# Agent attention and maxout FFN on one core: two key groups of the start turned another way, and the loads behind them

## The chip, the cores and the metric

The kernel runs on one NeuronCore of a Trainium2 chip. The metric is the device time of one execution in microseconds (us). Before the change the median of 12 runs is 464.67 us, from 464.09 to 465.64. The engines named below are TensorE (PE; PEld is its weight load), VectorE (DVE), ScalarE (ACT), GpSimd (POOL) and SyncE (SP), which here issues nearly all DMAs.

## What is computed

Agent attention is followed by a maxout feed-forward layer. Four batches have 12544 rows of 128 channels each; there are 49 agents a batch and 768 hidden units.

```python
a2k = sm(agents, k)          # softmax(scale * agents @ k^T)
agent_v = a2k @ v            # 49 x 128 for each batch
q2a = sm(q, agents)          # softmax(scale * q @ agents^T)
x = (q2a @ agent_v).reshape(B * S, D)
h = np.maximum(np.maximum(x @ w1, x @ w2), x @ w3)
return (h @ w_out).astype(np.float32)
```

Inputs and output are float32. The kernel works in bf16 on TensorE.

## The kernel before

Since `x` is a product with only 49 rows of `agent_v`, the kernel multiplies those by the weights first: for each batch it makes `G`, 49 rows wide enough for the hidden units, and every row of q then needs only its 49 exponentials times `G`.

**Stages.** Batch 0 has a pass of its own over its keys and values ("early" groups). After that the kernel runs over 49 q groups of 1024 rows, numbered s = 0 to 48. Most of the first 36 "host" a key group of the next batch: while q group s is worked through, up to 1152 rows of k and v (nine blocks of 128) are cast, scored and added up, so that `G` of the next batch is ready at its border. The last batch's q groups host nothing.

**A key group** (`k_group`) has these steps: `load` (k, then v, by SyncE, into one of 14 buffers called st), `cast_k` and `cast_v` to bf16 on GpSimd (L280, L287), `turn_k`, which transposes the keys, `scores` (L312, TensorE), `exps` (L317, ScalarE), `values` (L323, TensorE), and two additions. `turn_k` has two forms. The TensorE form writes nine transposes into a PSUM tile (L294), and `evacuate` copies that to the SBUF tile kT on VectorE (L300). The DMA form is one transposing DMA issued by SyncE (L296) from the cast keys k_bf to kT. Early groups and groups 0 to 2 take the TensorE form, all later ones the DMA form.

**A q group** (`q_group`) loads q (L474), casts it on GpSimd (L478), turns it on TensorE (L483) with a copy to qT (L489, VectorE; for group 0 half of it on ScalarE, L491), and makes scores (L504) and exponentials (L510). Then come six hidden slices, f = 0 to 5. For each, TensorE makes u (`first`) and v (`second`), both L530; ScalarE turns u to a (`relu_first`, L545); VectorE takes the maximum with v, called x (L555). Slice 3 works in one tile: ScalarE's a3 (L542) is written in place, v3 is added to it, and ScalarE makes the result (L553). In what follows u0 is u of slice 0, and so on. Last, TensorE multiplies by the output weights (L560, L569), VectorE scales (L576) and SyncE stores (L583).

**Order.** Each step is put on a list with a time of its own (`at`), in units of which a group has six; the tables `KEY`, `BEGIN` and others hold the offsets. `emit` sorts the list and issues in that order, holding a step back until what it needs has been issued. The order on every engine's queue, SyncE's included, follows from it. SyncE issues in order, so a DMA that waits for a cast holds up the loads behind it.

**The rings.** Hidden slices, products for `G` (L418, copied by L423 for batch 0) and the TensorE form of `turn_k` take turns in three PSUM buffers (ring "uv"). Scores, q turns, output tiles and some filler matmuls (L254, which keep TensorE busy) share two buffers of another ring ("om"). SBUF holds three each of k_bf, kT and q_bf.

`last_key` is the time of the last early group, -2.804. The step that turns the keys of hosted groups is set at the end of `k_group`:

Of the kernel before, what the change touches and what calls it, by code (L numbers as in the profile page):

```python
# [16 lines left out]
def kernel(  # L17
# [83 lines left out]
    def table(s):  # L101
        if s + 1 in tails:
            return BORDER
        return BEGIN if s in tails and s < SB else KEY if s < SB else LATE
# [6 lines left out]
    def uv_tile(dtype=FP32):  # L111
        return psum.tile([P, 2, 512 if dtype == FP32 else 1024], dtype, tag="uv", bufs=3, name="uv_ps")
# [6 lines left out]
    def at(key, fn, name=None, needs=(), ring=None, frees=()):  # L119

        ops.append((key, len(ops), fn, name, needs, ring, frees))
# [61 lines left out]
    def load_tile():  # L185
        return loads.tile([P, KT, C], FP32, tag="st", name="st")
# [77 lines left out]
    def k_group(b, t0, n, key, s):  # L264

        d = {}
        early = s is None
        K = None if early else table(s)
        if s == 0:
            key += BEHIND  # L270

        def load():
            for name, src in (("k", k), ("v", v)):
                t = d[name] = load_tile()
                nc.sync.dma_start(t[:, :n, :], src[b, t0 * P:(t0 + n) * P, :].rearrange(
                    "(p j) c -> p j c", j=n))

        def cast_k():
            d["kb"] = work.tile([P, KT, C], BF16, tag="k_bf", bufs=3, name="k_bf")
            nc.gpsimd.tensor_copy(out=d["kb"][:, :n, :], in_=d["k"][:, :n, :])  # L280

        def cast_v():
            d["vb"] = work.tile([P, KT, C], BF16, tag="v_bf", bufs=4, name="v_bf")
            if early:
                nc.scalar.activation(d["vb"][:, :n, :], d["v"][:, :n, :], AF.Copy)  # L285
            else:
                nc.gpsimd.tensor_copy(out=d["vb"][:, :n, :], in_=d["v"][:, :n, :])  # L287

        def turn_k():
            d["kT"] = work.tile([P, KT, P], BF16, tag="kT", bufs=3, name="kT")  # L290
            if early or s < 3:
                t = d["kT_ps"] = uv_tile(BF16).rearrange("p i c -> p (i c)")
                for j in range(n):
                    nc.tensor.transpose(t[:, j * P:(j + 1) * P], d["kb"][:, j, :], ident)  # L294
            else:
                nc.sync.dma_start_transpose(out=d["kT"][:, :n, :],  # L296
                                            in_=d["kb"][:, :n, :].rearrange("p j c -> p (j c)"))

        def evacuate():
            nc.vector.tensor_copy(out=d["kT"][:, :n, :].rearrange("p j c -> p (j c)"),  # L300
                                  in_=d["kT_ps"][:, :n * P])

        def scores():
            if early:
                d["pair"] = uv_tile()
                d["s"] = d["pair"][:, 0, :]
                last_tile["t"] = d["s"]
            else:
                d["s"] = host[s]
            t = d["s"]  # L310
            for j in range(n):
                nc.tensor.matmul(t[:, j * A:(j + 1) * A], d["kT"][:, j, :], agT[:, b, :A],  # L312
                                 start=(j == 0), stop=True, skip_group_check=True)

        def exps():
            d["e"] = work.tile([P, KT * A], BF16, tag="e_k", bufs=3, name="e_k")
            nc.scalar.activation(d["e"][:, :n * A], d["s"][:, :n * A], AF.Exp, scale=scale)  # L317

        def values():
            t, c = (d["pair"][:, 1, :], 0) if early else (d["s"], CV)  # L320
            for j in range(n):
                e = d["e"][:, j * A:(j + 1) * A]
                nc.tensor.matmul(t[:, c:c + A], d["vb"][:, j, :], e, start=(early and j == 0),  # L323
                                 stop=True, skip_group_check=True)
                if early:
                    nc.tensor.matmul(t[:, A:2 * A], ones_bf, e, start=False, stop=True,
                                     skip_group_check=True)

        def add_values():
            w = 2 * A if early else A  # L330
            src = d["pair"][:, 1, :w] if early else d["s"][:, CV:CV + A]
            if t0 + n == NT and not early:
                nc.vector.tensor_tensor(out=avT[:, b, :A], in0=src, in1=Vacc[b], op=ALU.add)
            elif t0:
                nc.vector.tensor_tensor(out=Vacc[b], in0=src, in1=Vacc[b], op=ALU.add)
            else:
                Vacc[b] = work.tile([P, w], FP32, tag=f"Vacc{w}", name="Vacc")
                nc.vector.tensor_copy(out=Vacc[b], in_=src)

        def add_exps():  # L340
            if t0:
                nc.gpsimd.tensor_tensor(out=Eacc[b][:, :n * A], in0=Eacc[b][:, :n * A],  # L342
                                        in1=d["e"][:, :n * A], op=ALU.add)
            else:
                Eacc[b] = work.tile([P, KT * A], FP32, tag="Eacc", name="Eacc")
                nc.gpsimd.tensor_copy(out=Eacc[b], in_=d["e"])

        if early:
            g = ("early", t0)
            at(key - 30, load)  # L350
            at(key - 5, cast_k)
            at(key - 4, cast_v)
            at(key, turn_k, ("kt", g), (), "uv", [("kt_out", g)])
            at(key + 0.5, evacuate, ("kt_out", g), [("kt", g)])

            last = [("normalise", 0)] if t0 + n == NT else []
            late = max(0, (key - last_key) / 6 + 2)
            at(min(key + 6.6, last_key + 0.58 + 0.02 * late), scores, ("ks", g), [("kt_out", g)],
               "uv", [("ka", g)] + last)
            at(min(key + 7, last_key + 0.64 + 0.01 * late), exps, ("ke", g), [("ks", g)])  # L360
            done = last_key + (0.6 + 0.1 * late if late >= 1 else 0.55)
            at(min(key + 13.2, done), values, ("kv", g), [("ke", g)])
            at(min(key + 13.6, done + 0.01), add_values, ("ka", g), [("kv", g)])
        else:
            at(6.0 * s - 24.6, load)
            at(max(6.0 * s - 12.6, last_key - 3.4 + 0.2 * s), cast_k, ("k_cast", s))
            at(max(6.0 * s - 10.6, last_key - 3.3 + 0.2 * s), cast_v, ("v_cast", s))
            if s > 2:
                at(max(key - 9.1, last_key - 3.2), turn_k, ("kt_out", s), [("k_cast", s)])
            else:  # L370

                turn = 6.0 * s - 3.3 if s else KEY["v0"] + 0.01
                at(turn, turn_k, ("kt", s), (), "uv", [("kt_out", s)])
                at(turn + 0.05, evacuate, ("kt_out", s), [("kt", s)])
            at(key + K["ks"], scores, ("ks", s), [("kt_out", s), ("ho", s)])
            at(key + K["ke"], exps, ("ke", s), [("ks", s)])
            at(key + K["ke"] + 1.5, add_exps, ("kx", s), [("ke", s)])
            at(key + K["kv"], values, ("kv", s), [("ke", s), ("v_cast", s)])
            at(key + K["ka"], add_values, ("ka", s), [("kv", s)])
# [71 lines left out]
    def q_group(s):  # L451
# [3 lines left out]
        key = 6.0 * s  # L455
# [132 lines left out]
        def put(name, fn, *needs, ring=None, frees=()):  # L588
            at(key + K[name] + (BEHIND if s == 0 and name in ("sum", "rec") else 0), fn, (name, s), needs,
               ring, frees)  # L590
# [3 lines left out]
        if s == 0:  # L594
            at(last_key - 29.9, load)
            at(last_key - 3.5, cast)
            at(last_key + 0.76, turn_q, ("qt", 0), (), "om", [("qe", 0)])
            at(last_key + 0.77, evacuate, ("qe", 0), [("qt", 0)])
            at(last_key + 0.94, scores, ("s", 0), [("qe", 0)], "om", [("ex", 0)])
            at(last_key + 0.941, exps, ("ex", 0), [("s", 0)])  # L600
        elif not q_dma:
            at(key - 26, load)
            at(max(key - 12.8, last_key - 3.45 + 0.2 * s), cast, ("q_cast", s))
            put("qt", turn_q, ("q_cast", s), ring="om", frees=[("qe", s)])
            put("qe", evacuate, ("qt", s), *([("s", s - 3)] if s >= 3 else []))
        else:
            at(key - 32, load)
            at(key - 14.3, cast)
            at(key - 12.3, turn_q_dma, ("qe", s))
# [46 lines left out]
    last_key = KEY["u0"] - 2  # L656
# [19 lines left out]
    for b in range(1, B):  # L676
        for g in range(NK):
            s = (b - 1) * NT // GT + g
# [41 lines left out]
```

The softmax here doesn't subtract the row's maximum and nothing guards it: scores larger than these inputs give would overflow.

## Time and profile before

| | |
|---|---|
| median of 12 runs | 464.67 us |
| the profiled execution | 464.82 us |
| its span, first to last instruction | 463.0 us |
| granted TensorE clock, mean | 0.999 |
| busiest groups: maximum (L555, VectorE) | 297.2 us, x245, 1221 ns each |
| ReLU (L545, ScalarE) | 240.8 us, x245, 1026 ns each |
| hidden slices (L530, TensorE) | 187.2 us, x1248 |
| DMA moved | 118.26 MB, mean 255 GB/s |
| key transposes by DMA (L296) | x30, median 5.2 us to landing |

All durations come from one profiled execution; the 1.8 us between its time and its span lie outside the first and last instruction. Busy shares are means over stages with different limits. Rows of a timeline give start, length, engine, line, operation, what it writes and reads, and in brackets how long the engine stood idle before it and what ended that. A row named SPq is the issue of a DMA; its landing is a separate time. "Issue" in the chain of waits is time in which the engine waited for nothing that the profile shows.

### The profile page before, as it was taken

How to read it: one execution, taken by the hardware profiler on the slowest of the kernel's cores; microseconds unless marked ns; L12 is line 12 of the kernel's file. 1: busy time of each engine (PE TensorE's matmuls, PEld its weight loads, DVE VectorE, ACT ScalarE, POOL GpSimd, SP SyncE). 2: the span in 40 equal slices, each digit the busy share in tenths (PEclk: the TensorE clock that was granted, in tenths of full speed). 3: DMA queues.
4: the chain of work that ended last, by engine and by line, in shares of the span. 5: the costliest groups of instructions: out<-in, count | busy, mean ns of one | idle time of the engine just before them, and what ended most of it. 6: DMA issues, size and time to landing. Idle time of an engine off the chain costs nothing.

```text
span 463.0 us, 13350 instructions
## 1 busy us (share of the span) xinstructions
PE 438.2 (95%) x5473; PEld 274.4 (59%) x5473; DVE 403.1 (87%) x512; ACT 396.2 (86%) x460; POOL 171.2 (37%) x179
## 2 busy tenths in 40 slices
PE   2597899999999999999999999999999999999995
PEld 2465466666665666666656666666656555555554
DVE  3255899999988999999989999999988999999995
ACT  3365889989899899899999998998999999999991
POOL 2244963553452545536272446353240101000000
PEclk9999999999999999999999999999999999999999
DMA  8999999996999899997997999986766486644122
GB/s 313 407 411 391 409 361 323 347 323 145 315 302 310 289 243 309 346 271 241 300 317 259 278 328 294 291 258 188 175 138 187 132 192 153 177 120 124 60 93 92
DMA packets 81449, 118.26 MB, mean 255 GB/s; under 512 B 55207, under 2 KB 56683, under 8 KB 81387
## 3 DMA queue, kind: packets, MB, share of 16 engines
q1 hardware_dynamic: 81184, 117.30, 82.4%
q8 instruction: 43, 0.70, 0.6%
q14 instruction: 19, 0.16, 0.1%
q10 hardware_dynamic: 203, 0.10, 0.1%
HBM read 78.74 MB, written 25.69 MB: 226 GB/s over the span
## 4 chain that ended last, share of the span: by engine, by line
PE 80%; DMA 8%; DVE 4%; ACT 4%; issue 2%; SPq 0%; POOL 0%; DVEq 0%; ACTq 0%
PE uv_ps L530 34%; PE o_ps L569 29%; PE o_ps L560 6%; DMA st<-in_k_dram 5%; PE m_ps L483 4%; PE m_ps L504 3%; DVE r L555 3%; ACT a_sb L545 2%; DMA st<-in_q_dram 2%; DMA st<-in_v_dram 2%; PE m_ps L323 2%; PE m_ps L312 1%; PE m_ps L518 1%; DVE o_sb L576 1%; ACT uv_ps L542 0%
## 5 line engine op out<-in xcount | busy, mean ns | idle before, releaser
L555 DVE TENSOR_TENSOR r<-uv_ps,a_sb 128x1024 bf16<-128x1024 f32 x245 | 297.2, 1221 | 14.7 <-PE uv_ps L530 6.5
L545 ACT ACTIVATE a_sb<-uv_ps 128x1024 bf16<-128x1024 f32 x245 | 240.8, 1026 | 14.9 <-PE uv_ps L530 13.6
L530 PE MATMUL uv_ps<-e_q,G 49*128 49x512 bf16 (+3 forms) x1248 | 187.2, 368 | 2.5 <-ACT uv_ps L542 0.7
L569 PE MATMUL o_ps<-wo_bf,r 128*128 128x128 bf16 x2352 | 175.3, 220 | 0.2 <-DVE r L555 0.2
L569 PEld LDWEIGHTS <-r 128*128 128x128 bf16 x2352 | 137.8, 98 | 40.1 <-issue 38.1
L530 PEld LDWEIGHTS <-G 49*128 49x128 bf16 x1248 | 57.8, 93 | 65.3 <-issue 33.2
L342 POOL TENSOR_TENSOR Eacc<-Eacc,e_k 128x441 f32<-128x441 f32 (+1 forms) x30 | 30.5, 1015 | 129.5 <-ACT e_k L317 129.5
L576 DVE TENSOR_TENSOR o_sb<-o_ps,recips 128x512 f32<-128x512 f32 x98 | 67.5, 689 | 9.2 <-PE o_ps L569 6.3
L478 POOL CAST q_bf<-st 128x1024 bf16<-128x1024 f32 x49 | 50.9, 1041 | 60.4 <-DMA qT<-q_bf 59.0
L553 ACT ACTIVATE r<-uv_ps 128x1024 bf16<-128x1024 f32 x49 | 50.2, 1024 | 18.0 <-PE uv_ps L530 17.7
L280 POOL CAST k_bf<-st 128x1152 bf16<-128x1152 f32 (+2 forms) x45 | 50.3, 1119 | 27.7 <-DMA st<-in_k_dram 20.9
L542 ACT ACTIVATE uv_ps<-uv_ps 128x1024 f32<-128x1024 f32 x49 | 49.6, 1012 | 1.6 <-issue 1.3
L560 PE MATMUL o_ps<-G,e_q 128*128 128x256 bf16 x196 | 38.0, 276 | 0.3 <-DVE o_sb L576 0.3
L287 POOL CAST v_bf<-st 128x1152 bf16<-128x1152 f32 (+1 forms) x33 | 37.5, 1135 | 0.6 <-DMA st<-in_v_dram 0.6
L510 ACT ACTIVATE e_q<-m_ps 128x512 bf16<-128x512 f32 x49 | 29.8, 608 | 0.5 <-PE m_ps L504 0.5
L300 DVE COPY kT<-uv_ps 128x1152 bf16<-128x1152 bf16 (+1 forms) x15 | 10.7, 713 | 16.6 <-PE uv_ps L294 16.6
L285 ACT ACTIVATE v_bf<-st 128x1152 bf16<-128x1152 f32 (+1 forms) x12 | 12.9, 1073 | 13.9 <-DMA st<-in_v_dram 13.9
L560 PEld LDWEIGHTS <-e_q 128*128 128x128 bf16 x196 | 12.4, 97 | 19.0 <-issue 17.8
L489 DVE COPY qT<-m_ps 128x1024 bf16<-128x1024 bf16 (+1 forms) x33 | 22.2, 673 | 0.8 <-PE m_ps L483 0.8
L483 PEld LDWEIGHTS <-q_bf 128*128 128x128 bf16 x264 | 14.9, 98 | 13.2 <-issue 10.6
L483 PE MATMUL m_ps<-ident,q_bf 128*128 128x128 bf16 x264 | 20.4, 220 | 0.5 <-POOL q_bf L478 0.5
L504 PE MATMUL m_ps<-qT,agT 128*64 128x512 bf16 (+3 forms) x104 | 19.9, 388 | 0.5 <-ACT qT L491 0.5
(71 smaller groups left out, 227.3 us busy)
## 6 DMA issues: line engine op xcount, KB each, us to landing
st<-in_q_dram SPq DMA_DIRECT2D x46, 512.0 KB, 5.3
out_dram<-o_sb SPq DMA_DIRECT2D x46, 512.0 KB, 3.2
st<-in_k_dram SPq DMA_DIRECT2D x40, 576.0 KB, 6.3
st<-in_v_dram SPq DMA_DIRECT2D x40, 576.0 KB, 7.6
st<-in_k_dram SPq DMA_DIRECT2D x3, 512.0 KB, 6.5
st<-in_v_dram SPq DMA_DIRECT2D x3, 512.0 KB, 7.4
wst<-in_moe_w_dram SPq DMA_DIRECT2D x3, 384.0 KB, 10.5
st<-in_q_dram SPq DMA_DIRECT2D x2, 384.0 KB, 5.0
```

The costliest lines, as they stand in the source:

```text
L280: nc.gpsimd.tensor_copy(out=d["kb"][:, :n, :], in_=d["k"][:, :n, :])
L287: nc.gpsimd.tensor_copy(out=d["vb"][:, :n, :], in_=d["v"][:, :n, :])
L478: nc.gpsimd.tensor_copy(out=d["qb"], in_=d["q"])
L483: nc.tensor.transpose(t[:, j * P:(j + 1) * P], d["qb"][:, j, :], ident)
L530: nc.tensor.matmul(t[:, h, j0 * P:j1 * P], G[b][h * H:h * H + A, col + f * P:col + (f + 1) * P], d["e"][h * H:h * H + A, j0 * P:j1 * P], s ...
L542: nc.scalar.activation(u, u, AF.Relu)
L545: nc.scalar.activation(a_sb[f], u, AF.Relu)
L553: nc.scalar.activation(r, v_ps[f], AF.Relu)
L555: nc.vector.tensor_tensor(out=r, in0=v_ps[f], in1=a_sb[f], op=ALU.max)
L560: nc.tensor.matmul(t[:, i * 2 * C:(i + 1) * 2 * C], d["e"][:, jj * P:(jj + 1) * P], G[batch[jj]][:, C1O:C1O + 2 * C], start=(i == 0), stop ...
L569: nc.tensor.matmul(t[:, c:c + C], r_sb[f][:, h, jj * P:(jj + 1) * P], wo_bf[:, f, :], start=False, stop=True, skip_group_check=True)
L576: nc.vector.tensor_tensor(out=d["out"][:, j:j + m, :], in0=d["o", o].rearrange("p (j c) -> p j c", c=C), in1=d["r"][:, j:j + m].unsqueeze( ...
```

## The change

Three things change. Group 0's keys are still turned on TensorE, but the step's time goes from 0.108 to `last_key + 1.05` = -1.754, ahead of the first hidden slices (u0 is at -0.804) and just behind the products for `G` (the second at -1.784). Group 2's keys are turned by DMA, at time 2.9, instead of on TensorE at 8.7; group 1's step keeps its time, 2.7. The loads of groups 4 and 5 move: q of 4 and 5 from -2 and 4 to 2.92 and 8.92, k and v from -0.6 and 5.4 to 2.95 and 8.95. That puts those of group 4 just behind the DMA transpose of group 2 (2.9), and those of group 5 just behind that of group 3 (8.9).

```diff
         def turn_k():
             d["kT"] = work.tile([P, KT, P], BF16, tag="kT", bufs=3, name="kT")
-            if early or s < 3:
+            if early or s < 2:
                 t = d["kT_ps"] = uv_tile(BF16).rearrange("p i c -> p (i c)")
...
-            at(6.0 * s - 24.6, load)
+
+            at(max(6.0 * s - 24.6, 6.0 * s - 21.05 if s in (4, 5) else -99), load)
             at(max(6.0 * s - 12.6, last_key - 3.4 + 0.2 * s), cast_k, ("k_cast", s))
             at(max(6.0 * s - 10.6, last_key - 3.3 + 0.2 * s), cast_v, ("v_cast", s))
-            if s > 2:
+            if s > 1:
                 at(max(key - 9.1, last_key - 3.2), turn_k, ("kt_out", s), [("k_cast", s)])
             else:
 
-                turn = 6.0 * s - 3.3 if s else KEY["v0"] + 0.01
+                turn = 2.7 if s else last_key + 1.05
                 at(turn, turn_k, ("kt", s), (), "uv", [("kt_out", s)])
...
         elif not q_dma:
-            at(key - 26, load)
+            at(key - (21.08 if s in (4, 5) else 26), load)
```

In the order of SyncE's queue that follows, the stretch q4, k4, v4, q5, k5, v5, transpose 3, q6 becomes transpose 2, q4, k4, v4, transpose 3, q5, k5, v5, q6 (a number is the group). On TensorE the nine transposes of group 0 stand ahead of u0, and u3 moves up to stand right behind v0; the nine of group 2 are gone, and so is one copy of kT on VectorE. GpSimd's order is unchanged.

## Prediction

> **What bounds the kernel now.** I read the busy shares and the slices first, then the chain of waits, then the timeline of the one stretch that the change touches.
>
> ```profile
> PE 438.2 (95%) x5473; PEld 274.4 (59%) x5473; DVE 403.1 (87%) x512; ACT 396.2 (86%) x460; POOL 171.2 (37%) x179
> ...
> PE   2597899999999999999999999999999999999995
> ...
> PEclk9999999999999999999999999999999999999999
> DMA  8999999996999899997997999986766486644122
> ```
>
> TensorE is full from the sixth slice on and its clock is granted throughout, so only its order of work counts there. The DMA engines are full up to about 104 us, so a transfer added there is not free of itself. What is shortened before TensorE fills up should shift everything behind it, as long as no load becomes late. Group s below means q group s, with the key group that it hosts. The chain of waits through the start (start, length, what) shows where it is not yet full:
>
> ```profile
> 46.93 0.33 PE uv_ps L530 x2
> 47.26 0.60 PE uv_ps L294 x9
> 47.85 1.30 issue
> 49.16 1.02 ACT uv_ps L542
> ...
> 60.70 0.52 PE uv_ps L294 x9
> 61.21 0.02 issue
> 61.23 0.76 DVE kT L300
> 61.99 0.61 DVE o_sb L576
> ```
>
> Both edits sit on the chain: the nine transposes of group 0's keys (47.26) with the ScalarE wait behind them, and the transposes of group 2's keys with their copy (60.70 to 61.99). The timeline gives the price of the second. The turn of q (L483) starts a period:
>
> ```profile
> 57.52 0.45 PEld L483 LDWEIGHTS <-q_bf 128*128 128x128 bf16 x8 [0.42 <-POOL k_bf L280]
> ...
> 66.91 0.45 PEld L483 LDWEIGHTS <-q_bf 128*128 128x128 bf16 x8 [0.42 <-issue]
> ...
> 75.26 0.45 PEld L483 LDWEIGHTS <-q_bf 128*128 128x128 bf16 x8 [0.42 <-issue]
> ```
>
> The period with the TensorE transposes lasts 66.91 - 57.52 = 9.39 us, the next, whose keys are turned by DMA, 75.26 - 66.91 = 8.35 us, as do those after it. The SyncE timeline shows the issue of a transpose in a full queue and in later ones:
>
> ```profile
> 57.18 5.19 SPq L296 DMA_TRANSPOSE kT<-k_bf  x1
> 62.81 0.35 SPq L474 DMA_DIRECT2D st<-in_q_dram  x1
> ...
> 67.35 2.11 SPq L296 DMA_TRANSPOSE kT<-k_bf  x1
> ```
>
> **Edit 1: group 0's keys turned earlier.** In the built order of instructions the nine transposes now stand between the products for G (L418) and the first slices u0 and u1 (L530); before, behind v0. No work goes or comes. The three buffers of the ring are passed on differently, so I follow the start event by event; starts and durations are rows of the timeline.
>
> - Transposes at 45.47, where u0 began. Nine take 0.52 to 0.60, so u0 begins at 46.0 instead of 45.47; its buffer, the first product's, is free by then (VectorE's second G copy ends at 45.95). a0 on ScalarE moves from 45.91 to 46.45.
> - u1 now takes the second product's buffer, free when the last G copy ends at 46.80 (45.25 + 1.55): u1 at 46.86 instead of 46.00, a1 at about 47.4.
> - The copy of kT (0.76) stands behind the G copies: 46.75 to 47.5 instead of 47.90 to 48.66. v0 takes its buffer: 47.54 instead of 46.87. Visible 0.39 later, it lets x0 start on VectorE at 47.96. Before, x0 stood behind the late kT copy, at 48.58. **Gain 0.62.**
> - u3 now comes right behind v0, at 47.76 instead of 48.68, where fillers, transposes and the q turn were ahead of it. a3 follows a1: 48.31 instead of 49.16. Gain 0.85, out of ScalarE's idle 1.31.
> - VectorE goes on in its old steps: qT of group 1 at 49.1 (49.71), x1 at 49.7 (50.31). Group 1's transposes wait for x1 to end: 50.95 instead of 51.57. u4 stands behind them, and a4 waits for u4: about 51.97 instead of 52.60. ScalarE was 0.85 early, but this wait leaves 0.62.
>
> From a4 on ScalarE's rows follow each other without a gap up to 57.6, so the step keeps about **0.6 us**. Bounds: 0.3, if u0 and u1, both late, cost ScalarE what they lose (0.54) and half comes back; 0.85, if a4 does not wait for u4. I take 0.6. The start's TensorE gaps stay below 0.5 us, as those of before, at a granted clock of 1.00; I charge nothing for the clock.
>
> **Edit 2: group 2's keys turned by DMA.** Nine transposes (0.52 on the chain) and one VectorE copy (0.76) go. In the period of 8.35 the same stretch has L569 x20 at 68.69 and L504 at 70.50, 1.81 apart; in that of 9.39 they are at 59.40 and 61.97, 2.57 apart. That is 0.76; the o_ps step (L560) then waits for the delayed o_sb copy, 0.67 behind L504 against 0.34: another 0.33. Together about the 1.04 by which the periods differ. What stays: the one-time copy of G (L249, 0.40), which makes L569 x20 start 1.88 after the turn against 1.78. So at most 0.94. And ScalarE comes late into this period: r3 (L553) starts 2.14 after the turn, against 1.72. Today the transposes cover those 0.42. Without them v4, which waits for a4 (in the later periods too, 71.54), may pass them on. So 0.5 to 0.94, with 1.04 as the outer bound; I take the middle, **0.75 us**.
>
> At this place a rule of the Trainium skill speaks against the edit: "VectorE: DVE Perf Modes", section "Rules for kernel authors", says to transpose 128x128 on TensorE if PSUM will do, and "The three transpose paths" puts 1.309 us on the DMA way. One block after another that is 9 x 1.309 = 11.8 us, an estimate. In this trace 30 such transposes of keys land 3.9 to 9.6 us after issue, median 5.2, queueing included. By the rule the keys would land at 53.0 + 11.8 = 64.8, by the rows at 56.9 to 62.6; what follows from each is worked out next.
>
> **The wait that comes in.** Group 2's DMA transpose waits for its cast on GpSimd, at 51.84 and 1.15 long, so it is issued at 53.0; k's load lands at 51.7 (40.84 + 10.9), which nothing in the change moves. It must land before the scores of group 2, now at 63.74, then at 63.74 - 1.35 = 62.4. Ahead of it in the queue stand only the loads issued up to 46.24, the last landing about 11 us later, at 57.2. The transpose issued at 57.18 met six loads issued later than those and still landed in 9.6. Group 2's meets 4.2 us of backlog: that one's was 65.6 - 57.2 = 8.4 (the v load of 54.51 plus 11.1), and it landed 1.2 behind it. So 57.2 + 1.2 = 58.4, 4.0 ahead of the need; the longest row, 9.6, gives 62.6, a loss of 0.2. I take zero.
>
> Behind it on SyncE wait q, k and v of group 4 (before at 47.67 to 50.36), then group 3's transpose (its cast ends at 57.15 as before) and q, k, v of group 5. The queue never runs dry: its backlog lasts to 57.2 and group 4's loads go out at about 55 to 56, after some 2.1 us of issue. In the queue they stand only behind the added transpose: landing 1.2 to 1.4 later, q of group 4 at about 59.9 (58.6 now), k at 61.3 (60.0). GpSimd's casts of them move from 59.17 and 60.15 to 60 and 61.4; the next on GpSimd is Eacc (L342), which stands idle 3.71 for ScalarE until 65.00, so it takes this. Group 3's transpose lands by about 64 to 66, needed at 72.10 - 1.35 = 70.7. Group 5's loads land by some 68.5 (65.6 now); their k goes through a cast at 68.04 into a transpose issued at 75.69. If it all came a further 5 us late (one more issue of 5.19), these gaps would just still hold it. Price: zero.
>
> **Sum.** 0.6 + 0.75 = 1.35 us off the profiled execution: 464.82 - 1.35 = 463.5 (span 463.0 to 461.6). The median of the runs is 464.67, 0.15 below the profiled one, so 463.3. Known bounds: 0.3 + 0.5 = 0.8 to 0.85 + 1.04 = 1.9, that is 463.9 to 462.8.
>
> **Rivals.**
>
> 1. *One of the two gains is swallowed* by the three-engine lock: ScalarE is already 86% busy, and what TensorE wins it waits for at a3 and a4. For it: the lag of 0.42, and u0, u1 and v0 all begin later than before (0.54, 0.86, 0.67). Against it: ScalarE has 0.54 and 0.18 of idle time in each period of 8.35. About 0.7 is left: 464.0; with nothing left, 464.7.
> 2. *Slower: the transpose lands late*, at the scores of group 2. TensorE stands there with all slices behind it, each us costs a us. It eats the gain from 62.4 + 1.35 = 63.75 on, and the kernel is slower by over 0.2% from 64.7, 11.7 after the issue. By the page's 1.309 a block, it lands at 64.8: 2.4 - 1.35 = +1.05, 465.7. For it: the queue is at 409 GB/s and full. Against it: none of the 30 rows reaches 9.7, and the backlog there is the smaller.
> 3. *The loads run late for good*: the added 1.2 us sits in a full queue up to 104 us. For it: the DMA row's nines. Against it: that row then drops to 6 and GB/s to 145, so the loads had got ahead. A late load would show as GpSimd waiting for st; from the waits in this stretch only the two early casts (2.2 in all) do. Time 464.7 to 466.
>
> **How the numbers follow.** About 0.2% (0.93 us) is what a measurement of this kernel tells from no change. Forecast 463.3: chance 0.66. Rival 1: 0.20, at 464.0, a third of it still over the bound. Rival 2: 0.08. Rival 3: 0.06, half of it no change. Of the forecast's own case some 0.05 falls within 0.2%, since its low end is 0.8. Faster 0.66 - 0.05 + 0.07 = 0.68, within 0.2% 0.05 + 0.13 + 0.03 = 0.21, slower 0.08 + 0.03 = 0.11. The range goes from 462.6, the upper bound of the gain with the runs' spread, to 464.8, which takes in rival 1.
>
> **What would show it.** Edit 1 right: the kT copy at about 46.8, a3 near 48.3 with ScalarE's 1.31 of idle time down to below 0.5, a4 near 52.0. Edit 2 right: no L294 behind 59, the period from the second to the third q turn (57.5 to 66.9) at 8.4 to 8.9. The wait right: SyncE's transpose at about 53.0, landing before 60, and no TensorE gap before the scores of group 2. Wrong would be: a gap there named after kT, casts waiting for st behind 60, or a period still above 9.

## The result, and the profile after

| | before | changed |
|---|---|---|
| median of the runs | 464.81 us (46 runs, 464.09 to 465.96) | 463.35 us (11 runs, 463.2 to 464.38) |
| ratio to before | | 0.9971, 95% interval 0.9963 to 0.9978 |
| the profiled execution, its span | 464.82, 463.0 us | 463.2, 461.4 us |

The changed kernel is 0.29% faster, 1.46 us in the median; 463.3 had been forecast. The page of the changed kernel gives the busy shares and, below, the 40 slices of the span:

```profile
PE 437.6 (95%) x5464; PEld 274.4 (59%) x5464; DVE 402.4 (87%) x511; ACT 396.0 (86%) x460; POOL 171.8 (37%) x179
...
PE   2598899999999999999999999999999999999996
...
PEclk9999999999999999999999999999999999999999
DMA  8999999999999999997987999996766566663222
```

Nine matmuls and one VectorE instruction are gone, and the granted clock is untouched. TensorE's row differs from that of before in two digits, so shares of the span can't tell where 1.5 us went; the stretch itself has to be read. The timeline of the turns of q, on TensorE's weight load (start, length, engine, line), shows the two periods that had been 9.39 and 8.35 us:

```profile
56.93 0.45 PEld L484 LDWEIGHTS <-q_bf 128*128 128x128 bf16 x8 [0.42 <-issue]
...
65.72 0.45 PEld L484 LDWEIGHTS <-q_bf 128*128 128x128 bf16 x8 [0.42 <-issue]
...
74.07 0.45 PEld L484 LDWEIGHTS <-q_bf 128*128 128x128 bf16 x8 [0.42 <-issue]
```

(In the changed kernel every line of the code from 365 on has a number one higher: L484 is the turn of q, L531 a hidden slice, L556 the maximum.) The period is now 65.72 - 56.93 = 8.79 us, and 8.35 follows. Since a start differs by some tenths from one execution to the next, everything below is counted from the first product for `G` on TensorE (its row in before, then in the changed kernel):

```profile
43.98 0.30 PE L418 MATMUL uv_ps<-wall,avT 128*64 128x256 bf16 x2
...
43.73 0.30 PE L419 MATMUL uv_ps<-wall,avT 128*64 128x256 bf16 x2
```

From there the span is cut at three more events. Each kernel was profiled twice:

| stretch (us) | before | before again | changed | changed again |
|---|---|---|---|---|
| start of the span to the first product | 43.98 | 44.17 | 43.73 | 44.29 |
| first product to a4 of group 0 | 8.62 | 8.61 | 8.29 | 8.29 |
| a4 to the turn of q of group 3 | 14.31 | 14.31 | 13.70 | 13.69 |
| that turn to the last maximum | 387.45 | 387.43 | 387.47 | 387.55 |
| last maximum to the end | 8.68 | 8.53 | 8.22 | 8.22 |

Row two is edit 1, row three edit 2: 0.33 and 0.61 us, and they repeat within 0.02. Row four, 84% of the span, hands both on unchanged. Row one is chance: two executions of one program differ by 0.56. Row five holds 0.3 to 0.5 us that no step of the prediction spoke of.

In the chain of waits of the changed kernel (start, length, what) the start reads:

```profile
46.60 0.39 PE uv_ps L531 x2
46.99 0.54 PE m_ps L254 x2
47.53 0.34 PE uv_ps L531 x2
...
47.97 1.23 DVE r L556
...
50.99 0.66 PE uv_ps L294 x9
51.65 0.34 PE uv_ps L531 x2
51.99 0.02 issue
52.02 0.68 ACT a_sb L546
```

The first three rows are u1, two filler matmuls (L254) and v0; x0 follows at 47.97, group 1's transposes at 50.99, u4 at 51.65 and a4 at 52.02. SyncE's timeline (a row is an issue, its length the time that SyncE spent on it) shows the new transpose, group 3's and group 4's:

```profile
52.97 1.34 SPq L296 DMA_TRANSPOSE kT<-k_bf  x1
54.37 0.64 SPq L475 DMA_DIRECT2D st<-in_q_dram  x1
...
57.10 2.28 SPq L296 DMA_TRANSPOSE kT<-k_bf  x1
...
66.16 6.56 SPq L296 DMA_TRANSPOSE kT<-k_bf  x1
```

They landed at 58.23, 65.60 and 77.81 us. GpSimd's timeline shows what the later loads cost its casts (L479 of q, L280 of k; in brackets the idle time ahead and what ended it):

```profile
67.00 1.04 POOL L479 CAST q_bf<-st 128x1024 bf16<-128x1024 f32 x1 [0.96 <-DMA st<-in_q_dram]
69.52 1.15 POOL L280 CAST k_bf<-st 128x1152 bf16<-128x1152 f32 x1 [1.48 <-DMA st<-in_k_dram]
```

Those are idle times of an engine that is busy 37% of the span.

### The profile page after: what moved, and what is told of

Same layout as the page of the kernel before. It is cut to its first block, busy times and chain, and to the rows that moved or that the text cites. A ratio compares the mean times of both kernels' runs of the same rounds, so it can differ in the third digit from the quotient of the medians.

```text
span 461.4 us, 13330 instructions
## 1 busy us (share of the span) xinstructions
PE 437.6 (95%) x5464; PEld 274.4 (59%) x5464; DVE 402.4 (87%) x511; ACT 396.0 (86%) x460; POOL 171.8 (37%) x179
## 4 chain that ended last, share of the span: by engine, by line
PE 80%; DMA 8%; DVE 5%; ACT 4%; issue 2%; SPq 0%; POOL 0%; DVEq 0%; ACTq 0%
PE uv_ps L531 34%; PE o_ps L570 29%; PE o_ps L561 6%; DMA st<-in_k_dram 5%; PE m_ps L484 4%; DVE r L556 4%; PE m_ps L505 3%; ACT a_sb L546 3%; DMA st<-in_q_dram 2%; DMA st<-in_v_dram 2%; PE m_ps L323 2%; PE m_ps L312 1%; PE m_ps L519 1%; DVE o_sb L577 0%; DVE G L424 0%
## 5 line engine op out<-in xcount | busy, mean ns | idle before, releaser
L556 DVE TENSOR_TENSOR r<-uv_ps,a_sb 128x1024 bf16<-128x1024 f32 x245 | 297.2, 1220 | 16.0 <-PE uv_ps L531 7.4
L531 PE MATMUL uv_ps<-e_q,G 49*128 49x512 bf16 (+3 forms) x1248 | 186.9, 368 | 2.4 <-DVE G L424 0.4
L531 PEld LDWEIGHTS <-G 49*128 49x128 bf16 x1248 | 57.9, 93 | 64.6 <-issue 32.8
L479 POOL CAST q_bf<-st 128x1024 bf16<-128x1024 f32 x49 | 50.9, 1040 | 61.9 <-DMA qT<-q_bf 59.1
L280 POOL CAST k_bf<-st 128x1152 bf16<-128x1152 f32 (+2 forms) x45 | 50.7, 1127 | 29.2 <-DMA st<-in_k_dram 25.5
L484 PEld LDWEIGHTS <-q_bf 128*128 128x128 bf16 x264 | 14.9, 98 | 13.2 <-issue 11.1
L484 PE MATMUL m_ps<-ident,q_bf 128*128 128x128 bf16 x264 | 20.5, 220 | 0.5 <-POOL q_bf L479 0.5
```

The lines of the kernel that those rows point to most:

```text
L479: nc.gpsimd.tensor_copy(out=d["qb"], in_=d["q"])
L484: nc.tensor.transpose(t[:, j * P:(j + 1) * P], d["qb"][:, j, :], ident)
L531: nc.tensor.matmul(t[:, h, j0 * P:j1 * P], G[b][h * H:h * H + A, col + f * P:col + (f + 1) * P], d["e"][h * H:h * H + A, j0 * P:j1 * P], s ...
L556: nc.vector.tensor_tensor(out=r, in0=v_ps[f], in1=a_sb[f], op=ALU.max)
```

## The experiments

All runs stand in one table, with the same cuts (the two together from the first product to the turn of group 3), so that a gain can be seen where it arises and where it gets lost.

| kernel | median us, ratio to before (95%) | a4 | q turn of group 3 | to last maximum | to the end |
|---|---|---|---|---|---|
| e1_group0 (edit 1 alone) | 464.64, 0.9997 (0.9989 to 1.0006) | 8.29 | 22.61 | 387.79 | 8.56 |
| e2_group2 (changed without edit 1) | 463.76, 0.9981 (0.9973 to 0.9990) | 8.61 | 22.30 | 387.61 | 8.22 |
| e3_oldloads (changed, loads at old times) | 463.50, 0.9974 (0.9964 to 0.9984) | 8.29 | 21.98 | 387.53 | 8.21 |
| e4_loads (loads' move alone) | 464.99, 1.0006 (0.9998 to 1.0015) | 8.61 | 22.92 | 387.42 | 8.56 |
| e5_gcopy (changed, copy of G on VectorE) | 463.58, 0.9976 (0.9967 to 0.9984) | 8.30 | 21.55 | 388.11 | 8.22 |
| e6_group1 (changed, group 1 by DMA too) | 469.69, 1.0111 (1.0098 to 1.0125) | 8.02 | 28.57 | 387.65 | 8.15 |
| e7_fetch_plus (changed, nine short matmuls more) | 464.05, 0.9985 (0.9976 to 0.9994) | 8.29 | 21.98 | 387.55 | 8.36 |
| e8_fetch_minus (before, ten fillers fewer) | 464.86, 0.9999 (0.9990 to 1.0008) | 8.62 | 22.93 | 387.57 | 8.29 |
| e9_nofill (changed, two fillers fewer) | 463.02, 0.9962 (0.9949 to 0.9975) | 8.09 | 21.80 | 387.56 | 8.22 |
| e10_both (e5 and e9 together) | 463.45, 0.9966 (0.9954 to 0.9979) | 8.10 | 21.35 | 388.11 | 8.23 |
| e11_again (changed again) | 463.27, 0.9967 (0.9958 to 0.9976) | 8.29 | 21.98 | 387.55 | 8.22 |
| e12_before_again (before again) | 464.62, 0.9995 (0.9985 to 1.0004) | 8.61 | 22.92 | 387.43 | 8.53 |

### The three parts one by one

Edit 1 alone, in the kernel before:

```diff
-                turn = 6.0 * s - 3.3 if s else KEY["v0"] + 0.01
+                turn = 6.0 * s - 3.3 if s else last_key + 1.05
```

> Edit 1 alone: group 0's keys turned ahead of u0 and u1, all else as before. Theory (two separate gains in the start, which add up): a3 follows a1 at once and ScalarE's idle time of 1.31 before it falls below 0.5; a4 is 0.3 to 0.6 us earlier, measured from the products for G (L418); the period from the second to the third q turn stays at 9.4; in all 0.3 to 0.6 us faster than before, about 464.3. Rival (the gains are one: what TensorE wins in group 0 is only kept because group 2's transposes go too): the 0.3 to 0.6 is waited away in group 1, the period there grows by as much, and the time is that of before within 0.2.

The changed kernel without edit 1 (group 0's keys turned behind v0 as before):

```diff
-                turn = 2.7 if s else last_key + 1.05
+                turn = 2.7 if s else KEY["v0"] + 0.01
```

> Everything of the change but edit 1: group 2's keys by DMA and the loads of groups 4 and 5 behind the transposes; group 0's keys at their old place. Theory: the start up to a4 as before (a3 behind 1.31 of idle ScalarE), the period from the second to the third q turn 8.8 instead of 9.4, in all 0.6 to 0.75 us faster than before, about 464.0. Rival (one gain): nothing or the whole 1.2 to 1.4.

The changed kernel with the loads of groups 4 and 5 at their old times:

```diff
-            at(max(6.0 * s - 24.6, 6.0 * s - 21.05 if s in (4, 5) else -99), load)
+            at(6.0 * s - 24.6, load)
...
-            at(key - (21.08 if s in (4, 5) else 26), load)
+            at(key - 26, load)
```

> Both turns as in the changed kernel, loads of groups 4 and 5 at their old times, so q, k and v of group 4 stand ahead of group 2's transpose on SyncE. Theory (the load move is there to keep that transpose from landing late): the backlog at 53 lasts to 61.4 instead of 57.2, the transpose lands at about 62.7, just behind the scores' slot of about 62.5; TensorE waits there 0.2 to 0.6 and that is lost: 463.6 to 464.0. Rival (the load move is worth nothing): as the changed kernel, 463.35. Other rival (the load move costs, since the loads of groups 4 to 6 run late behind it): faster than the changed kernel.

And that move of the loads alone, in the kernel before (the same two lines the other way round):

> Only the load move: both turns as before, q, k, v of groups 4 and 5 at their new times. Theory: as before within 0.2 us; in particular the 0.25 us by which the changed kernel's profile is earlier already at the products for G, and its last store's shorter landing (2.6 against 3.0), are chance and do not come back here in the median. Rival (part of the gain comes from the loads): 0.3 to 0.6 us faster.

Locally the parts add up exactly: e1 brings a4 from 8.62 to 8.29 and leaves the period behind at 9.40; e2 leaves a4 at 8.61 and has that period at 8.77; together they are the changed kernel's 21.99. In the medians they don't: edit 1 alone shows 0.16 us, not separable from nothing, and e2 shows 1.04, since it has the short end too (8.22; e1 and e4 have 8.56). The trace of e1 says where the 0.33 stays: the long middle stretch is 0.34 longer (387.79 against 387.45), which is taken up under the stalls below.

The loads' move is worth nothing either way. With the old order (e3) the three loads of group 4 are issued ahead of the transpose instead of behind it, and in SyncE's timeline its issue takes 5.28 us instead of 1.34:

```profile
52.93 5.28 SPq L296 DMA_TRANSPOSE kT<-k_bf  x1
58.27 0.57 SPq L475 DMA_DIRECT2D st<-in_q_dram  x1
```

It landed at 62.50 instead of 58.23, 9.57 us after its issue, while in e3's timeline of TensorE the scores that read it begin at 62.71: 0.2 us to spare, no loss, and the turn of group 3 at the same 21.98. So the move bought 4.3 us of margin at group 2 and no time. Delaying the loads cost no time either, but it cost margin further on: group 4's transpose lands 2.7 us ahead of its scores in e3 and 1.4 in the changed kernel.

### What took half of the expected gain of edit 2

> The changed kernel with the one-time copy of G (L249, 0.40 us) on VectorE instead of ScalarE. It measures the disputed cost of 0.43 that is left in the period of group 1 (8.78 from turn to turn against 8.35). Theory (ScalarE's lag, a3 and then a4 late, is what holds v4 up): a3 starts at the turn instead of 0.23 behind it, v4 no longer waits for a4, the period falls to 8.4 to 8.6 and the time by 0.2 to 0.4, to 463.0 to 463.15. Rival (the lag has another cause, the 0.86 us that r3 waits behind v3; or VectorE's x0 is late by as much): period and time stay within 0.1, or the period grows.

```diff
-        nc.scalar.activation(G[0][:, C1O:WC], linear["t"][:, C:3 * C], AF.Copy)
+        nc.vector.tensor_copy(out=G[0][:, C1O:WC], in_=linear["t"][:, C:3 * C])
```

In the changed kernel's timeline of TensorE one matmul pair waits in this period, v4 for a4:

```profile
61.99 0.39 PE L531 MATMUL uv_ps<-e_q,G 49*128 49x512 bf16 x2 [0.36 <-ACT a_sb L546]
```

With the one-time copy of `G` (L249, 0.41 us) on VectorE, u4 and v4 are one uninterrupted row in e5's timeline of TensorE:

```profile
61.54 0.82 PE L531 MATMUL uv_ps<-e_q,G 49*128 49x512 bf16 x4
```

The period falls from 8.78 to 8.33 us, the later ones' length. The lag of ScalarE behind TensorE was therefore that copy, and it is what kept edit 2 at 0.61 instead of about 1.04. The median does not follow (463.58, where 463.0 to 463.15 was expected): the middle stretch is 0.6 us longer. VectorE had room for the copy here, in its 0.66 of idle time before.

### What took half of the expected gain of edit 1

The changed kernel without the two filler matmuls between u1 and v0:

```diff
-    for key, n in fillers + [(last_key + 0.9, 2), (KEY["u1"] + 0.01, 2),
+    for key, n in fillers + [(last_key + 0.9, 2),
```

> The changed kernel without the two filler matmuls that stand between u1 and v0 of the first group on TensorE. Theory (edit 1 gained 0.33 us at a4 instead of the predicted 0.62 because, once group 0's keys are turned early, v0 waits behind these two fillers and no longer for anything of the group's own): v0 starts right behind the copy of kT, about 0.2 us earlier, and a4 stands at 8.05 to 8.1 us behind the first product matmul instead of 8.29; q's turn of group 2 at about 13.0 instead of 13.21; the median 463.1 to 463.2 if nothing far away answers. Rival (the chain of eviction and exponentials sets v0 and x0, the fillers lie in a gap): a4 stays at 8.25 to 8.35. A second rival: the fillers kept TensorE's clock up, and without them the products behind run longer: a4 later than 8.29.

In the changed kernel's timeline of TensorE, u1, the two fillers and v0 (in one row with u3) follow each other:

```profile
46.60 0.39 PE L531 MATMUL uv_ps<-e_q,G 49*128 49x512 bf16 x2 [0.39 <-DVE G L424]
46.93 0.61 PE L254 MATMUL m_ps<-busy,ident 128*128 128x512 bf16 x2
47.47 0.61 PE L531 MATMUL uv_ps<-e_q,G 49*128 49x512 bf16 x4
```

And in e9 (its origin lies 0.70 later than the changed kernel's):

```profile
47.31 0.39 PE L531 MATMUL uv_ps<-e_q,G 49*128 49x512 bf16 x2 [0.39 <-DVE G L424]
47.97 0.61 PE L531 MATMUL uv_ps<-e_q,G 49*128 49x512 bf16 x4 [0.27 <-DVE kT L300]
48.51 0.60 PE L254 MATMUL m_ps<-busy,ident 128*128 128x512 bf16 x2
```

Now v0 (second row, with u3) waits for the copy of kT, as the prediction had it, and starts 3.54 us behind the first product instead of 3.74. All of the 0.20 arrives at a4 (8.09) and at the turn of group 3 (21.80). Its median, 463.02, is the lowest of all, but its interval overlaps the changed kernel's; that the fillers cost 0.2 is shown by the trace, not by the medians.

Both of these edits together:

> As the run before, and the one-time copy into G on VectorE instead of ScalarE, which in an earlier run took 0.45 us off the period of group 2 but gave it back in small stalls of later groups. Theory: both gains stand near the start and add up, a4 at about 8.1 and q's turn of group 3 at about 21.3 us behind the first product matmul (changed kernel 21.99); the median about 462.7 if the far stalls stay as they are in the changed kernel, up to 463.5 if they fall as in that earlier run. Rival: the two are not additive, because without the fillers another wait ends last in group 2: q's turn of group 3 at 21.5 or later.

The gains add up where they arise (8.10 and 21.35 us; the forecast was 8.1 and 21.3). The median of 463.45 is not better, and again the middle stretch has 388.11.

### Stalls far from the change

> The changed kernel once more, with its profile. Theory: what the traces differ in far from the change (group 7's period of 8.48 us, group 22's of 9.14 or 8.98, the packet of instructions beside the last stores, the tail of 8.22) belongs to the program and repeats: the same group periods within 0.03 us, a tail of 8.2, no instruction packet beside the last stores. Rival: these come by chance from execution to execution, and at least one of them differs. The start (first product matmul at 43.73) is expected to differ by some tenths in either case.

> The kernel before once more, with its profile. Theory: its group periods repeat within 0.03 us (group 7 at 8.48), its tail is 8.6 to 8.7 with a packet of instructions beside the last stores, and its ratio is 1 within 0.1%. Rival: tail or periods differ from the first profile; then 0.46 us of the 1.63 us between the first two profiles were chance and not the change.

The periods of all 48 groups (first maximum to first maximum) repeat within 0.03 us between the two profiles of either kernel. So do the changed kernel's end of 8.22 and the missing packet of instructions; the end of before is 8.53 the second time, a little under the 8.6 to 8.7 expected. Between different kernels a few periods differ, far behind the edits, where the work and its order are the same. There are three patterns:

| group | before, changed, e3, e4, e7 to e9 | e1, e5, e10 | e2, e6 |
|---|---|---|---|
| 7 | 8.48 to 8.50 | 8.35 | 8.36 |
| 14 | 8.35 | 8.62 | 8.35 |
| 22 | 9.14 | 8.98 | 8.98 |
| 38 | 7.86 | 8.21 | 7.86 |
| first to last maximum of group 48 | 5.41 | 5.41 (e1), 5.69 (e5), 5.71 (e10) | 5.78 |

At the end of group 14, for one, a maximum starts 0.13 us after its releaser where those beside it that wait for ScalarE take 0.03 to 0.05, and the group then loses 0.27 (group 15 gives 0.06 of it back). For e10 these add up to 0.57, which is the 0.6 that its middle stretch is longer. So edits that change neither the work nor the order there move the end by up to 0.6 us, as fixed for one program as any other row. That explains why e1, e5 and e10 keep little of what they win. What it hangs on is open: small instruction packets of a queue of their own (q14) are read in groups 7, 22 and 38 of the changed kernel and of e5 alike, though in each of these groups only one of the two kernels stalls.

### The end of the kernel

The page's queue row and the chain's last row (start, length) of before:

```profile
q8 instruction: 43, 0.70, 0.6%
...
458.30 0.69 DVE o_sb L576
```

and of the changed kernel:

```profile
q8 instruction: 42, 0.69, 0.6%
...
457.12 0.69 DVE o_sb L577
```

From the last VectorE row to the end of the span (463.04 and 461.41) it is 4.05 us before and 3.60 after, with equal work. In between lie only the last two stores. In before one 16-KB packet of instructions is read beside them, and they land in 3.2 and 3.0 us (in its second profile 4.5 and 2.8); in the changed kernel that packet is missing and both land in 2.6. The short end goes with group 2's TensorE transposes gone: e2 and e3 have it, e1 and e4 do not. Two runs tried to move it: nine short matmuls added to the changed kernel at the start, and ten fillers fewer in the kernel before.

```diff
+    def short_matmuls():
+        t = small_tile("m_ps")
+        for _ in range(9):
+            nc.tensor.matmul(t[:, :64], ident, busy[:, :64], start=True, stop=True, skip_group_check=True)
+
+    at(first_key + 18.55, short_matmuls, "short", (), "om", ["short"])
```

> The changed kernel with nine short matmuls (64 columns, with their weight loads 18 instructions) added where TensorE stands idle at about 18 us, so that TensorE has as many instructions as before. The trace of before shows 43 packets of 16 KB on DMA queue 8 (instruction), the last at 458.9 beside the last stores, which land after 3.0; the changed one has 42 and 2.6. Theory (the shorter tail is the instruction fetch that is no longer needed): 43 packets again, 8.55 to 8.7 from the last maximum to the end instead of 8.2, 0.3 to 0.45 us slower than the changed kernel, about 463.75. Rival (the tail is short because of the added transpose or the order of DMA queues): 42 or 43 packets, tail 8.2, 463.35.

```diff
-            fillers += [(first_key + 6.0 * g + 0.55, 3), (first_key + 6.0 * g + 1.3, 3)]
+            fillers += [(first_key + 6.0 * g + 0.55, 2), (first_key + 6.0 * g + 1.3, 2)]
```

> The kernel before with ten filler matmuls (L254) fewer in the first pass, 20 TensorE instructions less; no key group is turned another way. Theory (instruction fetch): 42 packets on queue 8, tail 8.2 instead of 8.6 to 8.7, 0.3 to 0.45 us faster than before, about 464.4. If the clock were granted less without the fillers, the first pass would be longer, which shows as a later start of the products for G. Rival (the transpose makes the tail): tail and time as before.

Half an answer. With fewer instructions (e8) the packet goes and the tail is 8.29 instead of 8.53 to 8.68, with the nine transposes of group 2 still there; but its median is that of before, so as a gain of time this isn't shown. With more (e7) the tail stays short, against expectation: a 43rd packet is in the trace, but it starts at 462.78, behind the end of the span (462.48). The median of e7, 464.05, is 0.7 us above the changed kernel's all the same (0.3 to 0.45 was expected). In its profile that time lies ahead of the first product, which stands at 44.59, the latest of all; whether the nine matmuls did that or chance is not shown. Over all fourteen traces the rule holds without an exception: with the packet beside the stores 8.53 to 8.68, without it 8.15 to 8.36. Whether the packet lengthens the stores, or both have another cause, stays open.

### One group more

Group 1's keys turned by DMA too, in the changed kernel (`s < 1` and `s > 0` in place of `s < 2` and `s > 1`):

> The changed kernel with group 1's keys turned by DMA as well. Its cast ends at 49.1, so its transpose is issued then, behind a backlog that lasts to 57.2; it lands at about 58.4, while the scores of group 1 stand at 53.6. Theory (each us that a transpose is late costs a us): a TensorE gap of 4 to 5 us there, less the 1.0 that nine transposes and a copy cost, so 3 to 4 us slower than the changed kernel, 466.4 to 467.4. Rival (TensorE and the other engines catch part of it up, since the start is not full): less than 1.5 us slower, or no slower.

The waits of e6 between 48 and 66 us (who waited for what: us in all, times, longest):

```profile
PE m_ps L312 <- DMA kT<-k_bf: 5.2, 1, 5.2
```

and its windows (stretch, length, busy us and instructions of PE, PEld, DVE, ACT, POOL, then the granted clock, DMA share, GB/s):

```profile
52.00:56.00 4.00, 0.56 (x3) 0.19 (x2) 1.98 (x2) 1.82 (x3) 3.51 (x4) 0.74 1.32 369
56.00:60.00 4.00, 1.77 (x17) 0.79 (x17) 0.35 (x1) 0.54 (x1) 1.64 (x2) 0.50 0.91 233
60.00:64.00 4.00, 4.00 (x36) 2.48 (x35) 2.74 (x5) 3.39 (x5) 3.45 (x4) 0.50 1.02 335
64.00:68.00 4.00, 3.86 (x41) 2.06 (x39) 2.97 (x4) 2.69 (x3) 0.29 (x1) 0.98 1.13 344
```

This is the prediction's second rival, one group earlier. The transpose was issued at 49.00 and landed at 58.18, 9.2 us later. TensorE waited 5.2 for it and then worked on at a clock of 0.50 up to about 64. Four matmuls of a hidden slice show what that costs (in e6, then the same four in the changed kernel):

```profile
61.60 1.04 PE L531 MATMUL uv_ps<-e_q,G 49*128 49x512 bf16 x4
...
56.40 0.61 PE L531 MATMUL uv_ps<-e_q,G 49*128 49x512 bf16 x4
```

So the turn of group 3 comes 6.6 us later (28.57 against 21.98), although nine transposes and a copy are gone. In the median e6 is 6.3 us slower than the changed kernel; 3 to 4 was expected, with the gap but without the clock.

## Why the prediction was right, and where it was not

The time came out within 0.1 us, but not by its own sum: its two gains were put at 1.35 and measured 0.94. Of the 0.5 us between that and the measured 1.46, the end of the kernel gave 0.3 to 0.5, for which the sum had no term. That the total agrees so closely is luck.

**The wait that comes in, and its price of zero: right.** Issue at 53.0 (52.97), landing at 58.4 (58.23), TensorE without a gap at the scores. A sign named as "wrong" did appear, casts waiting for st behind 60, without harm: q and k of group 5 kept GpSimd idle for 0.96 and 1.48, and every period from group 3 on has its old length. That sign was badly chosen, since the prediction itself gave GpSimd room there. The cushion ahead is thinner than said, though: group 4's transpose took 6.56 to issue and landed 1.4 us before its scores (four to five us later loads were said to fit).

**The rule against the edit.** The prediction's estimate of 11.8 us took nine times the 1.309 us that the Trainium skill's page "VectorE: DVE Perf Modes", section "The three transpose paths", gives for one 128x128 block. For group 2 it was too long: its transpose landed 5.26 us after issue, and 9.57 in e3's fuller queue. Both lie inside the rows of the trace before (3.9 to 9.6), on which the prediction relied. But these rows were no upper bound: in the changed kernel itself group 4's transpose landed 11.64 us after its issue, and was in time only because its scores came later still. Over all the traces these transposes landed 3.7 to 11.8 us after issue, so no fixed time for each block describes them.

**Edit 1, 0.62 predicted, 0.33 measured: one term missing.** The copy of kT came when forecast (46.47 + 0.25 for the earlier origin = 46.72; 46.75 was said). The failed step is "v0 takes its buffer: 47.54". It looked at the buffer alone. On TensorE the two fillers follow u1, which the edit delays: u1 at 46.86, 0.33 for it and 0.54 for the fillers make 47.73, and 47.47 + 0.25 = 47.72 was measured. e9 takes the fillers out and gets v0 to 47.52 on the same origin, and 0.20 us back at a4. Another 0.08 stands between v0 and x0: x0 starts 0.50 behind v0 in the changed kernel and in e9, where the prediction put 0.42. Together that is 0.28 of the missing 0.29.

**Edit 2, 0.75 predicted, 0.61 measured: a size, inside its bounds.** The mechanism, a lag of ScalarE that v4 must wait for, is in the trace (0.36), and e5 shows its source, the one-time copy of `G`. Its being taken at the middle was the choice that missed; the whole lag is lost: 1.04 - 0.42 = 0.62. Two of its terms were loose besides. The pieces 0.76 and 0.33 make 1.09 and not the 1.04 of the periods; and the 0.10 taken off for the one-time copy is part of the same lag, since moving that copy gives back 0.44 in all (e5).

**Not in the sum: 0.3 to 0.5 us at the end.** The prediction let all work behind the edits shift unchanged. That held for the middle stretch (0.1 us at most), not for the last stores.

**The rivals.** Neither gain was swallowed whole (e1's and e2's traces have each in full). But the 0.94 that the two gained lies nearer to the first rival's 0.7 than to 1.35, and the lag of 0.42 that it named is what held edit 2 back. The late transpose did not come about, but e6 shows that it was one group away, and that there 5.2 us of waiting cost 6.6, more than the one us for each us of the prediction. Late loads did not decide (e3 against the changed kernel).

## What to carry to other kernels

When a step is moved, list what stands in the engine's own order between its new neighbours, fillers too: a buffer that comes free early helps only when the work queued ahead (0.54 us here) is done. A removed piece of work gives only what the next engine's lag leaves of it (0.61 of 1.04 here), so look for the one-time work that makes the lag. Where gains are tenths of a us, cut the trace at fixed events and compare the stretches, since a program's own stalls and its end can take or give as much as the edit.

## What the runs showed of the hardware

- A transposing DMA occupies SyncE while it is issued, for a time that depends on what is queued: 1.34 us for group 2's in the changed kernel, 5.28 for the same one with three more loads ahead (e3), 6.56 for group 4's. Over 14 profiles such transposes landed 3.7 to 11.8 us after issue. Loads behind it go out later by that much.
- A late operand can cost TensorE more than its lateness: after 5.2 us of waiting the granted clock was 0.50 for some 8 us, and the kernel lay 6.6 us behind (e6).
- The start up to the first product varied from 43.37 to 44.59 us over 14 profiles, by 0.56 for one and the same program: about as much as edit 2 gained.
- Stalls of 0.13 to 0.35 us in groups far from an edit repeat for one program within 0.03 us and differ between programs.
